# Two layers of long convolution and MLP: the first filter half loaded in quarters, the last MLP tile in two column pieces, and a new instruction order

## The chip, the cores and the metric

One core of one Trainium2 chip runs the whole program. The metric is device time in microseconds (us), lower is better. Engines: PE (TensorE), DVE (VectorE), ACT (ScalarE), POOL (GpSimd) and SP (SyncE, which here only issues DMAs).

## The reference, cut to what matters

```python
def _A_ref(q, k, v, shift_k, ssm_k, ssm_D):          # S = 2048 tokens, D = 512 channels
    for t in range(4):                                # a causal 4-tap filter along the tokens
        k_shift = k_shift + k_pad[:, t:t + S, :] * shift_k[:, 3 - t]
    kv = k_shift * v
    y = irfft(rfft(kv padded to 2S) * rfft(ssm_k padded to 2S))[:S]   # a long causal convolution per channel
    return q * (y + kv * ssm_D)

def _B_ref(x, w1, b1, w2, b2):                        # F = 1376
    return gelu(layernorm(x) @ w1 + b1) @ w2 + b2

x = A_q
x = x + _A_ref(layernorm(x), ...);  x = x + _B_ref(layernorm(x), ...)
x = x + _A_ref(layernorm(x), ...);  x = x + _B_ref(layernorm(x), ...)    # same weights
```

The convolution y does not depend on x, so it is computed once and used by both layers.

## The kernel before

The convolution is done as Fourier products by tables (Ft, Wt, Mt and Gt) on PE. Filter and input are cut into two halves of 1024 tokens, h = 0 and 1. A piece of work has a name, and the table ORDER lists all pieces, each with its engine (P for PE, A, D, G for POOL, S for SP) and its buffer (a PSUM slot 0 to 3 for a P piece). A piece is written out where the table puts it; each engine then runs its own pieces strictly in that order and waits by semaphores. A name that ends in e is the eviction from PSUM of the P piece before it, and the table says whether ACT or DVE does it. The pieces, with the half h as their first digit:

- lK: loads of the filter ssm_k (L391); KT: its transposes (L423); dt: adds ssm_D to one row. K0cSq: first stage of the filter's first half, 4 channel groups c by two parts q (L354); K0T: transposes of it (L368). The second half goes another way: K1S (L443), then K1w writes it to a buffer in DRAM and K1r reads it back regrouped (names zd; L382 and L388).
- lF, lW, lM, lG: loads of the tables Ft, Wt, Mt, Gt. lk: DMA transposes of the input k (L394). lv, lx, w1 to w4: loads of v, q and the weights.
- dg: diagonals for the 4-tap filter; kv: the filter as matmuls (L473); kvm: times v (DVE, L479).
- KW: second stage of the filter (L488); wa: a swap of its partitions by DMAs (L498). U0cSq, U0T and U1S, U1w, U1r: first stage of the input's two halves, made like the filter's. X: its second stage (L488). T, Ta, Tb: products with the filter on DVE (L547; they need X evicted, KW and wa). V: back transform (L558 for the first half, L572 for the second). The first half's V is transposed by TP (L589), the second's goes through DRAM (vw, vr). Y: the last stage (L603).
- For each of 8 token blocks i (two layers by four blocks of 512 tokens): sa and sb (statistics of the layernorm, DVE), pa, pb (its scale, POOL), aa, ab (applied, ACT or DVE), ga (gate by Y and sum, DVE), LT or dw and dr (transpose of the normed block on PE, or through DRAM by a DMA transpose, L674 and L677), m1 (first matmul of the MLP, L689), ge (gelu, ACT, L696), m2 (second matmul, four tiles of 128 tokens, 11 matmuls each, L706), re (sum with x, DVE, L710) and st (store, L719).

All DMAs named above go through SP's queue, one after the other; only of the last block's stores one half goes through ACT's queue.

At the start 38 matmuls on a zero tile (L322) keep PE busy while the first loads run.

Of the kernel before, what the change touches and what calls it, by code (L numbers as in the profile page):

```python
# [16 lines left out]
lK01.S lK00.S lF.S lG.S lK11.S lK10.S lk00.S KT01.P0 KT01e.D KT00.P1 dt1.D col.P0 KT00e.A K02S0.P2 cole.D K03S0.P3  # L17
K02S0e.D0 dg2.G KT11.P0 K03S0e.A1 K02S1.P1 KT11e.D lk01.S K03S1.P2 K02S1e.A KT10.P3 dt0.D dg1.G K03S1e.A K01S1.P1
KT10e.D K01S0.P0 K0T3.P2 K01S0e.A2 lv0.S K01S1e.D lW.S K00S0.P3 ones0.G K00S1.P0 lM.S dg0.G K00S0e.A1 K0T1.P1 lk10.S
K00S1e.D K0T3e.A K0T2.P3 K0T1e.D K0T0.P0 dg3.G K0T2e.D kv00.P2 K0T0e.A kv02.P1 kvm00.D kS.G KW03.P0 KW02.P3 kvm02.D  # L20
kv01.P2 KW02e.A lk11.S KW03e.A KW00.P1 kvm01.D U00S0.P3 KW00e.A KW01.P0 U00S0e.D1 kv03.P2 KW01e.A KW05.P1 kvm03.D
U02S0.P3 KW05e.A wa00.S U00S1.P0 U02S0e.A0 U03S0.P2 U00S1e.D U03S1.P1 U03S0e.A2 U01S0.P3 U03S1e.D U02S1.P0 U01S0e.A3
U01S1.P2 U02S1e.D KW06.P1 U01S1e.A KW07.P3 KW06e.D KW04.P0 U0T0.P2 KW04e.A U0T2.P1 KW07e.A U0T0e.D4 U0T1.P0 wa01.S
U0T2e.D5 X00.P2 X01.P3 U0T1e.D6 X00e.A U0T3.P1 X01e.A T00.D0 X02.P0 lx0.S K1S2.P2 X02e.A U0T3e.D0 X04.P3 w2.S K1S2e.A1
V00.P0 T01.D1 X06.P1 V00e.A X03.P2 X06e.D X03e.A X07.P0 X07e.A T02.D0 V01.P2 K1S6.P1 X04e.A T03.D1 V02.P0 V01e.A
K1S7.P3 T04.D0 K1S6e.A0 V03.P2 T06.D2 V02e.A X05.P1 X05e.A T07.D1 V04.P0 K1S7e.A V06.P1 T05.D0 V03e.A V07.P3 sa02.D
V06e.A V05.P2 lv1.S V07e.A K1S4.P1 sa10.D pa02.G K1w3.S V04e.A kv13.P3 sa00.D pa10.G V05e.A K1S5.P0 K1S4e.A5 TP01.P2
na02.D sa12.D pa00.G K1S5e.A TP00.P1 TP01e.A6 kvm13.D K1w2.S pa12.G TP02.P0 w1.S w3.S TP00e.D2 kv11.P3 TP02e.A0 aa00.D
Y01.P2 kv10.P1 kvm11.D aa02.A kv12.P0 kvm10.D Y01e.A Y00.P3 kvm12.D K1S0.P1 Y00e.A K1S3.P2 ga02.D K1S0e.A2 K1S1.P3
K1S3e.A ga00.D U1S0.P1 K1S1e.A TP03.P0 K1w1.S sb02.D U1S0e.A5 Y02.P3 K1w0.S w4.S U1S7.P2 Y02e.A sb00.D U1S6.P1 pb02.G  # L30
U1S6e.A0 U1S2.P3 TP03e.D6 pb00.G U1S7e.A U1S4.P1 ab02.D U1S2e.A1 U1S1.P0 U1w3.S K1r3.S ab00.D LT02.P2 U1S1e.A K1r1.S
na10.D LT02e.D LT00.P3 K1r0.S Y03.P0 na12.D aa10.A LT00e.D U1w0.S U1S3.P2 U1S4e.D6 m100.P3 U1S3e.A Y03e.D U1w1.S
U1S5.P2 ge00.A ga10.D m101.P1 aa12.A sb10.D m103.P3 ge01.A U1S5e.D pb10.G m102.P0 ge03.A ga12.D U1w2.S K1r2.S m104.P3
sb12.D ge02.A pb12.G KW16.P0 ge04.A m105.P2 KW16e.D U1r3.S6 KW10.P1 ge05.A KW11.P3 ab10.D KW13.P0 KW11e.A m201.P2
ab12.D dw10.S KW13e.A dw12.S U1r0.S1 KW10e.A KW15.P0 re01.D KW17.P3 KW15e.A KW14.P1 m200.P2 KW14e.D dr1.S KW17e.A
wa11.S X10.P3 re00.D KW12.P1 X16.P0 m203.P2 X16e.A0 sa20.D KW12e.A Tb16.D0 pa20.G X10e.A1 wa10.S m202.P1 Tb10.D1
re03.D m110.P3 aa20.D re02.D ga20.D m112.P1 ge10.A sa22.D U1r1.S5 m113.P3 ge12.A U1r2.S0 Ta16.D2 pa22.G lx1.S X11.P1
sb20.D V16.P2 X11e.A1 m114.P0 V16e.A1 Tb11.D0 pb20.G ge13.A aa22.D m111.P2 Ta10.D2 ge14.A nb20.D ga22.D V10.P3 ge11.A
X17.P0 Ta11.D1 m115.P1 V10e.A6 X12.P2 X17e.A1 Ta17.D2 V11.P3 X12e.A0 X14.P0 Tb17.D0 ge15.A X15.P2 Ta14.D1 X14e.A2
V17.P1 m210.P0 Tb14.D0 V17e.A X15e.A1 sb22.D vw13.S ab20.A V14.P2 Tb15.D2 pb22.G V11e.A m211.P1 Ta15.D0 V14e.A0 vw10.S  # L40
# [713 lines left out]
```

## Time and profile before

| | |
|---|---|
| time, three runs | 247.8, 247.82 and 248.97 us, median 247.82 |
| the profiled execution | 249.34 us, its span 247.6 us |
| busy in the span | PE 233.4, DVE 169.7, ACT 153.5, POOL 46.1 us |
| mean granted clock of PE | 0.989 |

The span runs from the first to the last instruction on the core; the time has some 1.7 us more around it. Matmuls overlap, so a PE that is shown busy need not be at its peak rate. Idle time of an engine is put down to whoever ended it. Of the lines numbered above, L266 is the eviction on ACT and L268 that on DVE.

### The profile page before, as it was taken

To read this page: it belongs to the slowest core of one execution; us is meant where nothing else is said; L and a number is where in the kernel's file an instruction comes from. 1 tells how busy PE (TensorE), PEld (TensorE's weight loads), DVE (VectorE), ACT (ScalarE), POOL (GpSimd) and SP (SyncE) were. 2 spreads that over 40 slices of the span, in tenths; PEclk is the share of its full clock that TensorE was granted. 3 is DMA by queue.
4 is the path that set the end of the run, shared out by engine and by line. 5 is a ranking of instruction groups with operands and counts; after the bars stand their busy time and mean duration, and the time that the engine had idled before them with its cause. 6 is when DMAs were issued, how large, how long until landed. Compare 5 with 4: busy or idle time off the path is not lost.

```text
span 247.6 us, 4645 instructions
## 1 busy us (share of the span) xinstructions
PE 233.4 (94%) x1852; PEld 122.7 (50%) x1852; DVE 169.7 (69%) x308; ACT 153.5 (62%) x197; POOL 46.1 (19%) x91
## 2 busy tenths in 40 slices
PE   8999997799899999988899999999999999999993
PEld 8997664585444344433343344444444444444441
DVE  0798899989998489999986996064886863001312
ACT  2678979989988745999329806794029521955000
POOL 1590000230202023304212550011132111000000
PEclk9999999999999999999799999999999999999998
DMA  6999979946599899936966152302401263300045
GB/s 211 263 265 243 206 160 220 376 160 230 217 274 360 255 232 207 290 67 184 230 196 211 45 127 96 75 3 85 86 0 45 77 134 88 82 3 0 0 115 139
DMA packets 41447, 38.72 MB, mean 156 GB/s; under 512 B 24556, under 2 KB 36306, under 8 KB 40402
## 3 DMA queue, kind: packets, MB, share of 16 engines
q1 hardware_dynamic: 41074, 38.17, 56.9%
q10 hardware_dynamic: 352, 0.27, 0.4%
q8 instruction: 14, 0.23, 0.4%
q14 instruction: 7, 0.06, 0.1%
HBM read 16.41 MB, written 12.06 MB: 115 GB/s over the span
## 4 chain that ended last, share of the span: by engine, by line
PE 78%; ACT 11%; DVE 5%; DMA 2%; issue 2%; POOL 1%; SPq 0%; DVEq 0%; ACTq 0%
PE p L689 31%; PE p L706 27%; ACT arena L266 10%; PE p L473 3%; PE p L368 3%; PE p L443 2%; PE p L572 2%; DMA arena<-zd 2%; DVE arena L268 2%; PE p L488 2%; PE p L322 2%; PE p L354 1%; PE p L423 1%; DVE arena L547 1%; PE p L589 1%
## 5 line engine op out<-in xcount | busy, mean ns | idle before, releaser
L266 ACT ACTIVATE arena<-p 128x1024 bf16<-128x1024 f32 (+1 forms) x79 | 79.8, 1103 | 15.5 <-PE p L488 6.1
L696 ACT ACTIVATE arena<-p,B 128x512 bf16<-128x512 f32 (+1 forms) x88 | 54.0, 686 | 43.6 <-PE p L689 43.5
L706 PE MATMUL p<-arena 128*128 128x512 bf16 (+1 forms) x352 | 78.9, 383 | 0.4 <-ACT arena L696 0.4
L689 PE MATMUL p<-arena 128*128 128x512 bf16 (+1 forms) x352 | 78.1, 379 | 0.0
L706 PEld LDWEIGHTS <-arena 128*128 128x128 bf16 (+1 forms) x352 | 34.2, 98 | 44.4 <-issue 4.7
L689 PEld LDWEIGHTS <-arena 128*128 128x128 bf16 (+1 forms) x352 | 34.7, 100 | 41.7 <-issue 1.9
L710 DVE TENSOR_TENSOR arena<-p,arena 128x512 bf16<-128x512 f32 x32 | 21.6, 685 | 43.6 <-PE p L706 24.1
L286 DVE BATCH_NORM_STATS2 lst<-arena 128x6 f32<-128x512 bf16 x64 | 40.8, 680 | 0.4
L293 POOL TENSOR_SCALAR lrs<-lmv 128x2 f32<-128x2 f32 x32 | 8.8, 276 | 148.6 <-DVE lmv L288 146.5
L547 DVE TENSOR_TENSOR arena<-arena 128x2048 bf16<-128x2048 bf16 x24 | 28.4, 1218 | 1.0 <-ACT arena L266 0.8
L304 ACT ACTIVATE arena<-arena,lnm,lrs 128x512 bf16<-128x512 bf16 x28 | 21.2, 809 | 11.9 <-DVE lnm L298 11.9
L295 POOL TENSOR_TENSOR lrs<-lrs,mhalf 128x2 f32<-128x2 f32 x32 | 25.9, 810 | 2.7
L655 DVE TENSOR_TENSOR arena<-arena 128x1024 bf16<-128x1024 bf16 x16 | 10.9, 681 | 13.8 <-ACT arena L304 11.8
L268 DVE COPY arena<-p 128x2048 bf16<-128x2048 bf16 (+1 forms) x13 | 14.5, 1136 | 8.2 <-PE p L423 6.6
L268 DVE CAST arena<-p 128x1024 bf16<-128x1024 f32 x14 | 16.7, 1217 | 1.8 <-PE p L488 0.9
L306 DVE TENSOR_SCALAR arena<-arena,lmv,lrs 128x512 bf16<-128x512 bf16 x36 | 13.1, 413 | 0.3 <-POOL lrs L295 0.2
L443 PE MATMUL p<-arena,Ft 128*128 128x512 bf16 x48 | 12.4, 380 | 1.0 <-ACT arena L266 0.7
L488 PE MATMUL p<-arena,Wt 64*64 64x512 bf16 x128 | 11.4, 391 | 1.9 <-ACT arena L266 1.0
L656 DVE TENSOR_TENSOR arena<-arena 128x1024 bf16<-128x1024 bf16 x16 | 11.1, 692 | 0.6
L572 PE MATMUL p<-arena 64*64 64x512 bf16 x128 | 9.0, 399 | 2.3 <-ACT arena L266 2.2
L456 POOL TENSOR_SCALAR arena<-IDt,sF 128x128 bf16<-128x128 bf16 x16 | 9.4, 604 | 7.6 <-DVE B L268 7.5
L479 DVE TENSOR_TENSOR arena<-p,arena 128x1024 bf16<-128x1024 f32 x8 | 9.6, 1222 | 1.6 <-PE p L473 1.4
(46 smaller groups left out, 123.1 us busy)
## 6 DMA issues: line engine op xcount, KB each, us to landing
arena<-arena SPq DMA_DIRECT2D x16, 256.0 KB, 4.1
zd<-arena SPq DMA_DIRECT2D x8, 512.0 KB, 5.2
arena<-zd SPq DMA_DIRECT2D x8, 512.0 KB, 5.9
lnd<-arena SPq DMA_DIRECT2D x14, 256.0 KB, 2.2
arena<-in_A_ssm_k_dram SPq DMA_DIRECT2D x4, 512.0 KB, 4.9
arena<-in_A_v_dram SPq DMA_DIRECT2D x2, 1024.0 KB
arena<-in_A_q_dram SPq DMA_DIRECT2D x4, 512.0 KB, 7.9
vd<-arena SPq DMA_DIRECT2D x8, 256.0 KB, 3.3
```

The costliest lines, as they stand in the source:

```text
L266: nc.scalar.activation(dst, src, AF.Copy)
L268: nc.vector.tensor_copy(dst, src)
L286: nc.vector.bn_stats(lst[:, i, :], xg[:, i, :])
L295: nc.gpsimd.tensor_tensor(self.rs[:, a:b], self.rs[:, a:b], mhalf[:, a:b], ALU.pow)
L304: nc.scalar.activation(dst[:, i, :], xg[:, i, :], AF.Identity, bias=self.nm[:, i:i + 1], scale=rs)
L443: nc.tensor.matmul(o[:, gh, :], Ft[:, t + gh, :], src[:, n, :], start=x == 0, stop=x == len(parts) - 1)
L488: nc.tensor.matmul(o[cols, par, :], Wt[rows, 2 * j + kk, :], z[rows, kk, :], start=True, stop=True)
L547: nc.vector.tensor_tensor(Tb[it["slot"]["T"]].rearrange("p s a d -> p s (a d)"), x2, kk, ALU.mult)
L689: nc.tensor.matmul(o[0:m, x, :], W1t[:, ct, ft * P:ft * P + m], lt[:, ct, :], start=ct == 0, stop=ct == CT - 1)
L696: nc.scalar.activation(ht[0:m, ft, :], o[0:m, x, :], AF.Gelu_apprx_tanh, bias=B1[0:m, ft:ft + 1])
L706: nc.tensor.matmul(o, ht[0:m, ft, t * P:t * P + P], W2t[0:m, ft, :], start=ft == 0, stop=ft == FT - 1)
L710: nc.vector.tensor_tensor(xg[:, t, :], view(pf[pe["slot"]["ps"]], [D]), xg[:, t, :], ALU.add)
```

## The change

1. The filter's first half comes in four loads of 128 channels (256 KB, before two of 512 KB), each with its own 8 transposes, its own eviction of 128x1024 and its own sum with ssm_D, so that a channel group of the first stage needs its own quarter alone.
2. The last block's tile t = 1 is made in two pieces of 256 columns, named x = 1 and x = 4, each with 11 matmuls, a sum and a store of its own. The piece of the first columns stands four tiles from the end, the other is the last of all.
3. 30 warm-up matmuls instead of 38.
4. A new table ORDER: other places for pieces on all engines, other engines for some evictions, and other PSUM slots.

```diff
-        for i in range(38):
+        for i in range(30):
             nc.tensor.matmul(pf[NPS - 1][:, 0:P], idle[:], idle[:], start=True, stop=True)
...
+        CW = [1, 2]
+        lK = [[load(f"lK{h}{x}", Kraw[h][:, x * CW[h]:(x + 1) * CW[h], :], ..., CW[h] << 18)
+               for x in range(CT // CW[h])] for h in range(2)]
...
+            w = CW[h]
+            for x in range(CT // w):
...
+                    for j in range(w):
                         for n in range(NT):
+                            nc.tensor.transpose(o[:, j, n, :], Kraw[h][:, w * x + j, n::NT], IDt[:])
...
-            zs = [first_stage("K0", Ktok[0], c, [KTe[0][c // 2]]) for c in range(CT)]
+            zs = [first_stage("K0", Ktok[0], c, [KTe[0][c]]) for c in range(CT)]
...
+            last = i == len(seq) - 1
+            for t, x, d0, d1 in [(0, 0, 0, D), (1, 1, 0, D // 2 if last else D), (2, 2, 0, D), (3, 3, 0, D)] + [(1, 4, D // 2, D)] * last:
+                def mms(it, t=t, ht=ht, d0=d0, d1=d1):
+                    o = view(pf[it["slot"]["ps"]], [d1 - d0])
...
+                        nc.tensor.matmul(o, ht[0:m, ft, t * P:t * P + P], W2t[0:m, ft, d0:d1], start=ft == 0, stop=ft == FT - 1)
...
+                def resid(it, pe=pe, xg=xg, t=t, d0=d0, d1=d1):
+                    nc.vector.tensor_tensor(xg[:, t, d0:d1], view(pf[pe["slot"]["ps"]], [d1 - d0]), xg[:, t, d0:d1], ALU.add)
...
+                            if d1 - d0 < D:
+                                o = apf(out, o.offset + d0, [list(o.ap[0]), list(o.ap[1]), [1, d1 - d0]])
+                                queue("A" if gh else "S").dma_start(o, xh[h][rows, n, d0:d1])
```

Of the table, one stretch on PE: the end of the second half's V pieces and the MLP tiles among them.

```diff
-V17.P1 m210.P0 Tb14.D0 ... V14.P2 ... m211.P1 ... V15.P2 X13.P3 ... V12.P2 ... V13.P2 m212.P3
+V17.P3 ... m211.P0 ... V14.P1 ... X13.P3 ... V15.P2 ab22.A m210.P1 ... V12.P2 re10.D ... V13.P2 m212.P1
```

First place, SP's queue from its first DMA to the swap of the first half. The names are those of the tensors: in_A_ssm_k is the filter, Ft, Gt, Wt and tabM the tables, in_A_k the input k, in_A_v the input v, and L498 the swap (wa). Before:

```order
L325 DMA arena<-in_A_ssm_k_dram 128x2x1024 x2
L325 DMA Ft<-tabF 128x768
L325 DMA Gt<-tabG 128x64
L325 DMA arena<-in_A_ssm_k_dram 128x2x1024 x2
L394 DMA_TRANSPOSE arena<-in_A_k_dram 128x4x512 x2
L325 DMA arena<-in_A_v_dram 128x4096
L325 DMA Wt<-tabW 128x1024
L325 DMA arena<-tabM 128x2048
L394 DMA_TRANSPOSE arena<-in_A_k_dram 128x4x512 x2
L498 DMA arena<-arena 32x4096 x8
```

The same stretch of SP's queue now, where the lines have moved by a few (L398 is the DMA transpose, L503 the swap):

```order
L326 DMA arena<-in_A_ssm_k_dram 128x1024 x4
L326 DMA Ft<-tabF 128x768
L326 DMA arena<-in_A_ssm_k_dram 128x2x1024 x2
L398 DMA_TRANSPOSE arena<-in_A_k_dram 128x4x512 x2
L326 DMA arena<-in_A_v_dram 128x4096
L326 DMA Wt<-tabW 128x1024
L398 DMA_TRANSPOSE arena<-in_A_k_dram 128x4x512
L326 DMA Gt<-tabG 128x64
L398 DMA_TRANSPOSE arena<-in_A_k_dram 128x4x512
L326 DMA arena<-in_B_b_dram 1x512
L326 DMA arena<-tabM 128x2048
L503 DMA arena<-arena 32x4096 x8
```

The filter's first half is four DMAs, Ft stands behind all four of them, and the table Mt (tabM) is moved from ahead of the second pair of transposes to the place right ahead of the swap.

Second place, DVE around the start of the MLP, from the eviction of the first block's second transpose (COPY 128x4x256, piece LT00e). CAST 128x1024 is an eviction, p0 to p3 the PSUM slots, L655 and L656 the gate, L286 and L288 statistics. Before:

```order
L268 COPY arena_63<-p3_156 128x4x256
L268 CAST arena_63<-p1_154 128x1024
L268 CAST arena_63<-p0_153 128x1024
L655 TENSOR_TENSOR arena_63<-arena_63 128x1024
L656 TENSOR_TENSOR arena_63<-arena_63 128x1024
L286 BN_STATS lst_87<-arena_63 128x6 x2
L288 BN_AGGR lmv3_97<-lst_87 128x2 x2
L268 CAST arena_63<-p2_155 128x1024
L655 TENSOR_TENSOR arena_63<-arena_63 128x1024
L656 TENSOR_TENSOR arena_63<-arena_63 128x1024
```

The same place now (L269 the eviction, L660 and L661 the gate):

```order
L269 COPY arena_63<-p0_153 128x4x256
L299 SCALAR_TENSOR_TENSOR lnm2_96<-lmv2_94,lrs2_95 128x2
L269 CAST arena_63<-p1_154 128x1024
L660 TENSOR_TENSOR arena_63<-arena_63 128x1024
L661 TENSOR_TENSOR arena_63<-arena_63 128x1024
L287 BN_STATS lst_87<-arena_63 128x6 x2
L289 BN_AGGR lmv3_97<-lst_87 128x2 x2
L660 TENSOR_TENSOR arena_63<-arena_63 128x1024
L661 TENSOR_TENSOR arena_63<-arena_63 128x1024
```

Three evictions (U1S4e, Y03e, U1S5e) have left this place for ACT, and one (Y02e) has come.

Third place, DVE's last five rows, the sums of the last tiles. Before:

```order
L710 TENSOR_TENSOR arena_63<-p2_155,arena_63 128x512 x2
L710 TENSOR_TENSOR arena_63<-p3_156,arena_63 128x512
L710 TENSOR_TENSOR arena_63<-p0_153,arena_63 128x512 x2
L710 TENSOR_TENSOR arena_63<-p3_156,arena_63 128x512
L710 TENSOR_TENSOR arena_63<-p2_155,arena_63 128x512
```

And now:

```order
L717 TENSOR_TENSOR arena_63<-p3_156,arena_63 128x512 x2
L717 TENSOR_TENSOR arena_63<-p2_155,arena_63 128x512
L717 TENSOR_TENSOR arena_63<-p0_153,arena_63 128x256
L717 TENSOR_TENSOR arena_63<-p3_156,arena_63 128x512
L717 TENSOR_TENSOR arena_63<-p0_153,arena_63 128x256
```

The last sum is of 256 columns, and the other piece of that tile stands one row ahead of the last whole one.

125 lines of the change are left out of this document (59 added, 66 removed).

## The prediction

> **What bounds the kernel now.** I read the page first (shares and clock), then the busy time by stage, then the chain of work that ended last, and then the timeline at the places where the chain leaves PE.
>
> ```profile
> span 247.6 us, 4645 instructions
> PE 233.4 (94%) x1852; PEld 122.7 (50%) x1852; DVE 169.7 (69%) x308; ACT 153.5 (62%) x197; POOL 46.1 (19%) x91
> ```
>
> The 94% of PE is a mean over stages. The next view cuts the span where the chain changes; each row gives a stretch, its length, and busy us (and instructions) of PE, weight loads, DVE, ACT and POOL, then the granted clock, the DMA share and GB/s.
>
> ```profile
> 20.87:49.89 29.02, 25.06 (x477) 16.96 (x476) 27.91 (x32) 27.00 (x30) 1.79 (x4) 1.00 0.96 234
> 49.89:69.42 19.53, 18.61 (x206) 12.13 (x205) 17.82 (x36) 18.50 (x20) 3.52 (x8) 1.00 0.58 203
> 69.42:80.75 11.33, 11.33 (x63) 5.00 (x62) 10.25 (x18) 9.61 (x16) 1.76 (x4) 1.00 0.92 315
> 80.75:118.85 38.10, 34.79 (x273) 14.71 (x271) 33.23 (x51) 29.25 (x36) 8.11 (x8) 1.00 0.83 206
> 118.85:138.67 19.82, 19.39 (x99) 7.84 (x98) 16.80 (x42) 11.06 (x18) 6.07 (x12) 0.91 0.66 190
> 138.67:243.41 104.74, 104.73 (x484) 47.59 (x483) 51.07 (x118) 46.15 (x73) 14.02 (x29) 1.00 0.26 66
> 243.41:247.60 4.19, 0.00 (x0) 0.00 (x0) 0.69 (x1) 0.00 (x0) 0.00 (x0) 0.76 0.43 127
> ```
>
> From 138.67 on PE runs 484 MLP matmuls without a gap, 104.74 us, 0.216 each. No order makes that shorter. What can move is the time at which PE reaches that stretch, and the 4.19 us behind it. Ahead of it DVE and ACT are the full engines: from 20.87 to 49.89 they are busy 27.91 and 27.00 of 29.02, and from 20.87 to 118.85 DVE works 27.91 + 17.82 + 10.25 + 33.23 = 89.2 of 98.0 us. DVE's last product of the convolution (piece Tb13) ends at 118.85, and the last V piece starts on PE 0.06 later, as the chain (start, length, what) shows:
>
> ```profile
> 1.05 4.24 PE p L322 x38
> 5.28 1.62 PE p L423 x16
> ...
> 8.54 1.04 PE p L354 x8
> 9.57 0.99 PE p L423 x16
> ...
> 116.73 1.08 PE p L572 x16
> ...
> 118.91 1.59 PE p L572 x16
> 120.51 5.96 PE p L706 x22
> ...
> 138.67 9.67 PE p L706 x44
> ```
>
> So I read the change by one question: when does DVE finish Tb13, and does PE then run through.
>
> **Term 1, the head (filter loads and first stage).** Rows of the timeline (SP's issues, the first 4-tap products on DVE, the first second-stage matmuls on PE) and of the DMA issues (size, us from issue to landing):
>
> ```profile
> 1.81 0.47 SPq L325 DMA_DIRECT2D Ft<-tabF  x1
> 14.08 0.42 SPq L325 DMA_DIRECT2D Wt<-tabW  x1
> 19.35 2.36 DVE L479 TENSOR_TENSOR arena<-p,arena 128x1024 bf16<-128x1024 f32 x2 [0.60 <-PE p L473]
> 20.14 0.63 PE L488 MATMUL p<-arena,Wt 64*64 64x512 bf16 x8
> ...
> Wt<-tabW SPq DMA_DIRECT2D x1, 256.0 KB, 5.6
> Ft<-tabF SPq DMA_DIRECT2D x1, 192.0 KB, 4.9
> ```
>
> Now the first stage starts at 8.54, after 16 transposes (1.62), their eviction and the corner sum. With quarters, 30 warm-ups of 4.24 / 38 = 0.11 end at 4.4 and 8 transposes at 0.1 end at 5.2; but the first stage also needs Ft. Ft lands at 1.81 + 4.9 = 6.7, behind 1 MB of filter in both orders. Four quarters of transposes and their first evictions fill PE until about 7.3, so the first stage starts some 1.2 earlier. Two more evictions and corner sums on DVE cost 0.2 of it, which leaves 1.0 for the 4-tap products on DVE (19.35). The second stage gets less: Wt lands at 14.08 + 5.6 = 19.7, the same bytes ahead of it, and PE starts it at 20.14 now, so its lead cannot pass 0.45. I take -0.6; bounds 0 and -1.0. The 8 warm-ups taken out (0.9 us of PE) are inside this: the landing of the loads covers them.
>
> A page's rule on these warm-ups: the Trainium skill, "TensorE: Matmul & The Clock Gate", section "Part 1: The HAM clock gate (the "warmup" mystery)", says PE starts at half rate and is released after a free-running window of about 3.4 us of sustained work. The rows agree so far: the first 16 transposes take 1.62, a later 16 take 0.99. By that rule 30 warm-ups alone would be too short to fill a window, and the sum would be -3.4 instead of -4.0 if the loads leave a hole; in the sum itself nothing of this is used.
>
> **Term 2, work taken off DVE.** By the order, between the first 4-tap product and Tb13 DVE loses three evictions net: one in the input's first stage (five became four) and two at the start of the MLP (of five, three left and one came, and one of KW's moved between engines both ways). The sum of one MLP tile (piece re10) is moved ahead of Tb13. Prices:
>
> ```profile
> 26.95 3.47 DVE L268 CAST arena<-p 128x1024 bf16<-128x1024 f32 x3
> ...
> L710 DVE TENSOR_TENSOR arena<-p,arena 128x512 bf16<-128x512 f32 x32 | 21.6, 685 | 43.6 <-PE p L706 24.1 <-ACT arena L696 19.5
> L479 DVE TENSOR_TENSOR arena<-p,arena 128x1024 bf16<-128x1024 f32 x8 | 9.6, 1222 | 1.6 <-PE p L473 1.4
> L268 DVE COPY arena<-p 128x1024 bf16<-128x1024 bf16 x2 | 1.4, 688 | 0.0
> ```
>
> Three evictions in a row take 3.47; one sum 0.69: -3.47 + 0.69 = -2.8. DVE was idle 98.0 - 89.2 = 8.8 in this stretch, and I leave that as it is; if it grows by as much as was taken off, the term is 0, and if the better fit also takes a third of the idle time away, it is -5.7. I take -2.8, because the row that it rests on is the full engine's own. What hides the three evictions on ACT is ACT's idle time: 98.0 - (27.00 + 18.50 + 9.61 + 29.25 = 84.4) = 13.6.
>
> The next one late could be a DMA. The second half's X pieces wait at 87.15 for the input read back from DRAM:
>
> ```profile
> 82.08 0.59 SPq L388 DMA_DIRECT2D arena<-zd  x1
> 87.15 0.84 PE L488 MATMUL p<-arena,Wt 64*64 64x512 bf16 x12 [0.47 <-DMA arena<-zd]
> ...
> 74.09 1.20 DVE L268 CAST arena<-p 128x1024 bf16<-128x1024 f32 x1
> ```
>
> That read is issued at 82.08, after SP has stored the block's normed rows. The last eviction of the input's first stage (74.09 on DVE, U1S5e) is one of those that are moved ahead of the MLP, and the two gates behind it on DVE come sooner by the evictions taken out, so this DMA moves with DVE and does not keep the gain.
>
> **Term 3, behind Tb13.** Between 115 and 125 the clock falls:
>
> ```profile
> 115.00:120.00 5.00, 2.80 (x47) 1.28 (x36) 5.00 (x7) 3.62 (x5) 0.00 (x0) 0.93 0.70 208
> 120.00:125.00 5.00, 5.00 (x24) 1.84 (x17) 5.00 (x15) 1.02 (x1) 2.64 (x6) 0.73 0.99 240
> ```
>
> PE has 2.20 idle here, and then 16 V matmuls take 1.59 instead of 1.08 and 22 MLP matmuls 5.96 instead of 9.67 / 2 = 4.84: 1.6 lost to the clock. Now an MLP tile (piece m210, 11 matmuls, 9.67 / 4 = 2.4) stands between the V pieces there, ahead of the two that wait longest. If that keeps the clock up, up to 1.6 is won. But something else is late next. The following block's normed rows come by a DMA transpose:
>
> ```profile
> 143.76 1.87 SPq L677 DMA_TRANSPOSE arena<-lnd  x1
> arena<-lnd SPq DMA_TRANSPOSE x7, 4.3
> ```
>
> It lands at 143.76 + 4.3 = 148.1, and PE begins that block at 138.67 + 9.67 = 148.3. There is no slack, so PE can gain behind Tb13 only what that chain gains, and DVE, which carries it, is busy 16.80 of 19.82. I take -0.7, near the middle of 0 and -1.6. The same page and section say that the rate falls back after a whole idle window; here PE was busy 2.80 of the 5.00 us and the clock fell all the same (0.93, then 0.73), so the row decides; by the page there would be no dip to remove, and the sum would be -3.3.
>
> **Term 4, the end.** The last sum is on 256 columns. The rows for 512 and 1024 columns (685 and 1222 ns) give 537 ns per 512, so 256 cost 685 - 268 = 417: -0.27. The split adds 11 matmuls but no columns (8 of 256 columns take 1.04 with their tail, 0.11 each, half of 0.216). The store is half as large; it lands 2.5 after its issue now, and for its size I count nothing.
>
> ```profile
> out_dram<-arena ACTq DMA_DIRECT2D x4, 64.0 KB, 2.5
> ```
>
> I take -0.3; bounds -0.2 and -0.4.
>
> **Term 5, a wait added.** The table Mt now stands ahead of the swap in SP's queue.
>
> ```profile
> 24.66 3.14 SPq L498 DMA_DIRECT2D arena<-arena  x4
> 34.41 1.22 DVE L547 TENSOR_TENSOR arena<-arena 128x2048 bf16<-128x2048 bf16 x1
> ...
> arena<-arena SPq DMA_DIRECT2D x16, 256.0 KB, 4.1
> ```
>
> The swap lands at 24.66 + 3.14 + 4.1 = 31.9, and the first product on DVE needs it at 34.41, which terms 1 and 2 (one eviction of the three) move to about 32.7. Mt's 512 KB at 234 GB/s (stage row) are 2.2 us. If all of that comes ahead of the swap, it lands at 34.1 and DVE waits 1.4; but the transposes of k no longer queue behind Mt and all of the bytes are the same, so most is given back. I take +0.4; bounds 0 and +1.4. The q load behind the swap is in this too.
>
> **Sum:** -0.6 - 2.8 - 0.7 - 0.3 + 0.4 = -4.0. The profiled execution took 249.34 with its span of 247.6, so it would become 245.3; it lies 1.5 above the median of the runs, 247.82, which would become 243.8.
>
> **The rivals.**
> - *The added wait and the DMA chain take most of it.* Term 5 in full (+1.0 more) and term 3 at 0 (+0.7): -2.3, 245.5. For it speaks the DMA share of 0.96 in the stage, against it that the bytes do not change. A late clock release at the head (0.6 lost, 244.4) lies on the way to it.
> - *The new order does not do what it says:* DVE's idle time grows by what was taken off, and Wt stops the head. Then the end and a part of the head stay: 247.82 - 0.3 - 0.4 = 247.1. The 8.8 idle us are made of many short waits, which another order can as well make longer.
> - *Slower: ACT becomes the engine that sets the first MLP.* The evictions taken off DVE, and the second normed pair of the next block, now stand on ACT ahead of the first gelu:
>
> ```profile
> 71.35 1.27 ACT L696 ACTIVATE arena<-p,B 128x512 bf16<-128x512 f32 x2 [0.66 <-PE p L689]
> 72.50 1.51 ACT L304 ACTIVATE arena<-arena,lnm,lrs 128x512 bf16<-128x512 bf16 x2
> ```
>
>   ACT is busy 18.50 of 19.53 from its last V eviction (49.89) to the first MLP matmul. The three evictions, priced as on DVE, and the pair are 3.47 + 1.51 = 5.0 more ahead of the gelu. Free are 1.03 there and the 0.66 that the first gelu waits. The pair is no longer between the gelus, 1.5 back. If ACT gets to its last V eviction at the old time, PE reaches the second matmul 5.0 - 1.7 - 1.5 = 1.8 later, and the end is at 247.82 + 1.8 - 0.3 = 249.3. It decides when ACT's lead at that eviction is under 1.5. Against it: ACT was idle 2.0 from 20.87 to 49.89 (29.02 - 27.00), and the head's lead arrives there.
>
> **How the numbers follow.** A difference under 0.5% (1.24 us) cannot be told from no change. Forecast, 241.9 to 244.9, chance 0.56. The wait and the chain, 244.9 to 246.6, 0.20. Only a rest stays, 246.6 to 249.0, 0.15. ACT bound, above 249.0, 0.09. Faster than 246.6: 0.56 + 0.20 = 0.76; within, 0.15; slower, 0.09. The low end is term 2 at -3.8 and term 3 at -1.6 with the others as taken, -5.9: 241.9. The high end, 247.1, is where the third case is half held; above it lie about 0.16, below the low end about 0.04.
>
> **What would show it.** DVE's last product (the last L547 row, now L552) ends near 115.4 instead of 118.85; no row of clock under 0.9 between 110 and 125; the stretch of MLP matmuls without a gap begins near 135 and is as long as before; the last sum takes 0.42; the first stage begins near 7.3. Wrong would be: a first product on DVE waiting for the swap by over 1 us, ACT without a gap up to a first gelu later than 71, or PE idle for a DMA transpose behind 138.

## The result, and the profile after

The changed kernel takes 246.48 us (median of 5, 246.03 to 246.93), the kernel before 248.47 on the same chip (median of 5): a ratio of 0.9899, 95% interval 0.9863 to 0.9935. Medians are of all executions; ratios, here and below, leave out those more than 1.5% above the fastest of their kernel. The profiled execution of after took 246.79.

The head of its page, and its time by stage (start:end, length, busy us and instructions of PE, weight loads, DVE, ACT and POOL, granted clock, DMA share, GB/s), cut at the same events as before:

```profile
span 245.1 us, 4654 instructions
...
PE 230.9 (94%) x1855; PEld 122.6 (50%) x1855; DVE 165.1 (67%) x308; ACT 156.8 (64%) x202; POOL 46.9 (19%) x91
```

```profile
22.22:50.25 28.03, 25.33 (x476) 16.84 (x472) 25.68 (x27) 27.13 (x30) 0.68 (x2) 1.00 0.92 237
50.25:70.28 20.03, 18.33 (x214) 12.75 (x213) 19.20 (x41) 19.45 (x21) 4.64 (x11) 1.00 0.71 249
70.28:81.18 10.90, 10.90 (x62) 4.79 (x60) 9.08 (x19) 10.65 (x18) 3.19 (x5) 1.00 0.87 301
81.18:118.53 37.35, 35.05 (x273) 14.77 (x271) 32.63 (x50) 29.17 (x36) 8.05 (x8) 1.00 0.86 215
118.53:136.72 18.19, 17.75 (x98) 7.49 (x98) 17.01 (x45) 11.05 (x18) 6.02 (x12) 1.00 0.67 187
136.72:241.49 104.77, 104.76 (x495) 48.73 (x494) 50.47 (x114) 46.57 (x73) 13.99 (x29) 1.00 0.30 69
241.49:245.10 3.61, 0.00 (x0) 0.00 (x0) 0.43 (x1) 0.00 (x0) 0.00 (x0) 0.91 0.23 55
```

DVE is busy 4.6 less than before and ACT 3.3 more: the evictions that changed engine (of those of 128x1024 f32, DVE does 10 instead of 14 and ACT 78 instead of 74). The gapless MLP stretch starts at 136.72 instead of 138.67 and is as long as before (104.77 and 104.74). The first row starts 1.35 later than before, at 22.22. The fifth row is 1.63 shorter and has a clock of 1.00 where it had 0.91. The last is 0.58 shorter.

The timeline of after, at the head and at the end (start, length, engine, line, what, and in brackets how long the engine sat idle and for what):

```profile
0.80 1.86 SPq L326 DMA_DIRECT2D arena<-in_A_ssm_k_dram  x4
...
4.50 10.56 SPq L398 DMA_TRANSPOSE arena<-in_A_k_dram  x2
...
7.08 0.60 PE L355 MATMUL p<-Ft,arena 128*128 128x256 bf16 x4
...
15.11 0.58 SPq L326 DMA_DIRECT2D arena<-in_A_v_dram  x1
...
21.11 3.73 DVE L484 TENSOR_TENSOR arena<-p,arena 128x1024 bf16<-128x1024 f32 x3 [1.60 <-DMA arena<-in_A_v_dram]
...
241.52 0.43 DVE L717 TENSOR_TENSOR arena<-p,arena 128x256 bf16<-128x256 f32 x1 [0.51 <-PE p L713]
241.97 0.53 SPq L728 DMA_DIRECT2D out_dram<-arena  x1
```

The first stage starts on PE at 7.08, before at 8.54. But the first 4-tap product on DVE starts at 21.11, before at 19.35, and DVE has waited 1.60 for v. SP issued v at 15.11, before at 13.44, since the two DMA transposes of k ahead of it took 10.56 of the queue; before they took 8.07. The same two rows before:

```profile
5.33 8.07 SPq L394 DMA_TRANSPOSE arena<-in_A_k_dram  x2
...
13.44 0.58 SPq L325 DMA_DIRECT2D arena<-in_A_v_dram  x1
```

From that product to the gapless stretch after needs 136.72 - 21.11 = 115.61, before 138.67 - 19.35 = 119.32. So the profiles differ by +1.76 at the head, -3.71 in the middle and -0.58 at the end.

### The profile page after: what moved, and what is told of

Read it like the earlier page. It is cut to its first block, busy times and chain, and to the rows that moved or that the text cites. A ratio compares the mean times of both kernels' runs of the same rounds, so it can differ in the third digit from the quotient of the medians.

```text
span 245.1 us, 4654 instructions
## 1 busy us (share of the span) xinstructions
PE 230.9 (94%) x1855; PEld 122.6 (50%) x1855; DVE 165.1 (67%) x308; ACT 156.8 (64%) x202; POOL 46.9 (19%) x91
## 4 chain that ended last, share of the span: by engine, by line
PE 77%; DVE 6%; DMA 5%; SPq 5%; ACT 4%; issue 2%; DVEq 0%; ACTq 0%
PE p L713 31%; PE p L694 31%; SPq L398 4%; DVE arena L552 4%; PE p L478 3%; ACT arena L267 3%; PE p L448 2%; DMA arena<-in_A_v_dram 2%; PE p L577 2%; PE p L493 2%; DMA zd<-arena 2%; PE p L369 1%; PE p L594 1%; PE p L355 1%; DMA arena<-in_A_ssm_k_dram 1%
## 5 line engine op out<-in xcount | busy, mean ns | idle before, releaser
L267 ACT ACTIVATE arena<-p 128x1024 bf16<-128x1024 f32 (+2 forms) x84 | 83.3, 1098 | 13.2 <-PE p L493 5.7
L713 PE MATMUL p<-arena 128*128 128x512 bf16 (+3 forms) x363 | 77.8, 373 | 0.5 <-ACT arena L701 0.4
L694 PE MATMUL p<-arena 128*128 128x512 bf16 (+1 forms) x352 | 77.9, 380 | 0.0
L713 PEld LDWEIGHTS <-arena 128*128 128x128 bf16 (+1 forms) x363 | 35.1, 97 | 42.3 <-issue 2.6
L694 PEld LDWEIGHTS <-arena 128*128 128x128 bf16 (+1 forms) x352 | 34.8, 100 | 41.6 <-issue 2.0
L717 DVE TENSOR_TENSOR arena<-p,arena 128x512 bf16<-128x512 f32 (+1 forms) x33 | 21.5, 667 | 49.9 <-PE p L713 39.0
L294 POOL TENSOR_SCALAR lrs<-lmv 128x2 f32<-128x2 f32 x32 | 10.0, 314 | 145.8 <-DVE lmv L289 141.9
L269 DVE COPY arena<-p 128x2048 bf16<-128x2048 bf16 (+1 forms) x14 | 14.9, 1070 | 10.5 <-PE p L428 7.2
L660 DVE TENSOR_TENSOR arena<-arena 128x1024 bf16<-128x1024 bf16 x16 | 10.9, 683 | 4.4 <-ACT arena L305 2.5
L269 DVE CAST arena<-p 128x1024 bf16<-128x1024 f32 x10 | 12.0, 1217 | 2.0 <-ACT arena L701 1.6
L661 DVE TENSOR_TENSOR arena<-arena 128x1024 bf16<-128x1024 bf16 x16 | 11.1, 692 | 0.6
```

The lines of the kernel that those rows point to most:

```text
L267: nc.scalar.activation(dst, src, AF.Copy)
L269: nc.vector.tensor_copy(dst, src)
L694: nc.tensor.matmul(o[0:m, x, :], W1t[:, ct, ft * P:ft * P + m], lt[:, ct, :], start=ct == 0, stop=ct == CT - 1)
L713: nc.tensor.matmul(o, ht[0:m, ft, t * P:t * P + P], W2t[0:m, ft, d0:d1], start=ft == 0, stop=ft == FT - 1)
L717: nc.vector.tensor_tensor(xg[:, t, d0:d1], view(pf[pe["slot"]["ps"]], [d1 - d0]), xg[:, t, d0:d1], ALU.add)
```

## The experiments

Every profile below is read by the same two marks: the start of the first 4-tap product (the head) and the distance from it to the gapless stretch (the middle). "Ratio" is to the kernel before on the same chip.

**The three evictions back on DVE.**

```diff
-U1S4e.A1 ... U1S5e.A ... Y03e.A
+U1S4e.D1 ... U1S5e.D ... Y03e.D
```

> The changed kernel with the three evictions U1S4e, U1S5e and Y03e done by DVE again instead of ACT. Theory 1 (term 2: DVE is the full engine, each eviction of 1.16 on it is on the path): DVE's last product of the convolution ends 1.5 to 3.5 later than 118.53, the gapless MLP stretch starts 1.5 to 3.5 later than 136.72, and the time is 248.0 to 250.0. Theory 2 (ACT is as full, so that what DVE loses ACT had gained): the last product ends within 0.7 of 118.53, and the time stays at 246.0 to 247.2.

Measured: 249.47, ratio 1.0044 (1.0022 to 1.0067), 3.0 more than after. Its timeline and its chain of work:

```profile
20.45 2.36 DVE L484 TENSOR_TENSOR arena<-p,arena 128x1024 bf16<-128x1024 f32 x2 [1.13 <-DMA arena<-in_A_v_dram]
...
119.80 1.21 DVE L552 TENSOR_TENSOR arena<-arena 128x2048 bf16<-128x2048 bf16 x1
```

```profile
137.88 1.27 ACT arena L701 x2
139.15 0.04 issue
139.20 0.81 PE p L713 x3
```

The last product starts 2.48 later than in after (117.32), with a head 0.66 sooner. The middle is 139.20 - 20.45 = 118.75, 3.14 longer than in after, for three evictions priced at 3.47. Theory 1 holds: they stood on the path, and ACT had room for them. The clock is not the cause: seven of the twelve executions have a mean clock of 0.992 or less, but the other five, at 0.998 or more, have a median of 249.28.

**The MLP tile as a filler, alone in the kernel before.**

```diff
-V14.P2 Tb15.D2 pb22.G V11e.A m211.P1 Ta15.D0 ... vw12.S V12.P2
+V14.P2 Tb15.D2 pb22.G V11e.A Ta15.D0 ... vw12.S m211.P1 V12.P2
```

> The kernel before with one MLP tile (piece m211, 11 matmuls, 2.4 us on PE) moved from ahead of the V piece V14e's neighbour to right ahead of V12, so that PE has work while DVE makes the last products. Theory 1 (term 3: the clock drop behind Tb13 comes from PE's idle time of 2.2 us ahead of it): the clock rows of 115 to 125 rise from 0.93 and 0.73 to 0.98 or more, and the gapless stretch starts 1.0 to 1.6 sooner than 138.67, at 137.1 to 137.7; the time falls by as much from 248.5. Theory 2 (the drop has another cause, or the DMA transpose of the next block sets the end of this stretch anyway): the stretch starts within 0.5 of 138.67 and the time stays within 0.5 of the kernel before, whether or not the clock rises.

Measured: 248.82 against 248.68, ratio 1.0005 (0.9977 to 1.0033). In its profile the clock does rise, by the time in 5-us windows:

```profile
115.00:120.00 5.00, 3.82 (x38) 1.77 (x41) 4.45 (x6) 3.41 (x4) 0.00 (x0) 1.00 0.73 213
120.00:125.00 5.00, 4.95 (x33) 2.12 (x23) 5.00 (x14) 1.03 (x1) 2.62 (x6) 1.00 1.02 219
```

Its gapless stretch starts at 137.53, 1.14 sooner than in the profile of before. The times do not follow, as theory 2 has it for the time, while the stretch starts where theory 1 has it. The next experiment shows why.

**The four loads alone, in the kernel before.** The first half comes in four loads with four transposes and sums; nothing else moves.

```diff
-lK01.S lK00.S lF.S lG.S lK11.S lK10.S lk00.S
+lK02.S lK03.S lK00.S lK01.S lF.S lG.S lK11.S lK10.S lk00.S
```

> The kernel before with the filter's first half in four loads, its transposes in four pieces, and nothing else changed (the order of the rest, the 38 warm-up matmuls' successor count and the tail as before). Theory 1 (the four loads slow what stands behind them): the second filter half lands at 11.8 or later instead of 10.6, the first 4-tap product starts 1.0 or more later than 19.1 to 19.4, the time grows by 0.5 to 1.5 from 248.5. Theory 2 (quarters alone cost nothing behind them): it starts within 0.4 of 19.2, and the time stays within 0.6 of the kernel before.

Measured: 248.91 against 248.08, ratio 1.0033 (1.0002 to 1.0064). Timeline at the head, then the same 5-us windows:

```profile
5.63 7.75 SPq L396 DMA_TRANSPOSE arena<-in_A_k_dram  x2
...
19.11 2.35 DVE L482 TENSOR_TENSOR arena<-p,arena 128x1024 bf16<-128x1024 f32 x2 [0.61 <-PE p L476]
```

```profile
115.00:120.00 5.00, 2.79 (x52) 1.32 (x44) 5.00 (x6) 3.91 (x5) 0.00 (x0) 1.00 0.72 211
120.00:125.00 5.00, 5.00 (x31) 2.20 (x24) 5.00 (x14) 1.02 (x1) 2.65 (x6) 1.00 1.05 225
```

The head is at 19.11: four loads in the old order delay nothing at the head, as theory 2 has it. The time is 0.83 longer, which is theory 1's range; this profile has no place for that loss, and it stays unexplained. And PE is busy 2.79 of 5.00, as in the profile of before, with no filler, yet the clock stays at 1.00. The middle is 137.67 - 19.11 = 118.56. Its chain shows what comes next when the clock does not fall: PE gets through to 126.65 and then waits for the second half's V, read back from DRAM.

```profile
126.65 3.89 DMA arena<-vd
```

**The split last tile alone, in the kernel before,** its two pieces as the last two.

```diff
-m270.P0 st23.S st73.S m271.P2 re70.D st51.S re72.D st70.S st72.S re71.D st71.S
+m270.P0 st23.S st73.S m271.P2 re70.D st51.S re72.D st70.S st72.S m274.P3 re71.D st71.S re74.D st74.S
```

> The kernel before with its last MLP tile alone in two pieces of 256 columns, the second of them the last of all, and nothing else changed. Theory 1 (term 4 as predicted: only the shorter last sum counts): the stretch behind the last matmul is 3.9 instead of 4.19, and the time falls by 0.3. Theory 2 (the smaller store lands sooner too, as the changed kernel's profile shows): it is 3.5 to 3.7 and the time falls by 0.5 to 0.7. Theory 3 (the split costs PE as much, 11 more matmuls of half the columns with a gap): the gapless stretch is 0.3 or more longer and the time does not change.

Measured: 248.92 against 248.08, ratio 1.0025 (1.0000 to 1.0051). By windows, and by the timeline of the end:

```profile
115.00:120.00 5.00, 2.79 (x40) 1.39 (x36) 5.00 (x7) 3.58 (x5) 0.00 (x0) 0.90 0.72 211
120.00:125.00 5.00, 5.00 (x25) 1.81 (x18) 5.00 (x15) 1.02 (x1) 2.65 (x6) 0.76 0.98 234
...
243.72:247.70 3.98, 0.00 (x1) 0.00 (x0) 0.42 (x1) 0.00 (x0) 0.00 (x0) 1.00 0.37 105
```

```profile
242.36 1.36 PE L707 MATMUL p<-arena 128*128 128x256 bf16 x11 [0.17 <-DVE arena L711]
...
243.76 0.42 DVE L711 TENSOR_TENSOR arena<-p,arena 128x256 bf16<-128x256 f32 x1 [1.11 <-PE p L707]
244.25 1.18 SPq L722 DMA_DIRECT2D out_dram<-arena  x2
```

Behind the last matmul 3.98 are left, not 3.61. The two stores of 32 KB stand one after the other on SP (1.18), so the second waits for the first, and PE waits 0.17 for a buffer. The stretch behind the last matmul is near theory 1's 3.9, but the gapless stretch is 0.35 longer (138.63 to 243.72), and the time does not fall: theory 3. The changed kernel has the first piece four tiles from the end; that place alone, in the old order, was not run.

**Mt back behind Wt.**

```diff
-lW.S dg0.G ... KW00e.A lM.S U02S0.P1
+lW.S lM.S dg0.G ... KW00e.A U02S0.P1
```

> The changed kernel with the load of Mt moved back to its old place, right behind Wt and ahead of the last two DMA transposes of k. Theory 1 (term 5 of the prediction: Mt ahead of the swap delays it): the swap lands up to 0.4 sooner, the first product of the convolution starts by 36.0 instead of 36.33, and the time falls by 0.4 or less. Theory 2 (the swap is held by the evictions of the filter's second stage, not by Mt): the swap is issued at 27.0 as now and the time stays within 0.3 of 246.5. Theory 3 (the DMA queues are full from 20 to 27): the last transposes of k, now behind Mt, come later, and the time grows by up to 1.0.

Measured: 246.26, ratio 0.9914 (0.9883 to 0.9945). The first issues of the swap (timeline), first in this version:

```profile
27.09 3.14 SPq L503 DMA_DIRECT2D arena<-arena  x4
```

And in after:

```profile
27.01 3.28 SPq L503 DMA_DIRECT2D arena<-arena  x4
```

Mt ahead of the swap costs nothing: in after Mt is issued by 25.57, and the swap comes 1.44 later, when an eviction on ACT is done. Here the queue is not free before 26.97, since the transposes of k come later. The first product is 0.45 sooner (35.88), which theory 1 has too, but only because the head is (20.65): from the head to it are 15.23, in after 15.22. So it is theory 2, with the queue in the place of the evictions in this one version.

**Plain loads ahead of the DMA transposes of k.**

```diff
-lK11.S lk00.S ... lk01.S ... lv0.S ... lW.S
+lK11.S lv0.S lW.S lk00.S lk01.S
```

> The changed kernel with two lines of SP's queue moved: the plain loads of v and Wt stand ahead of the two DMA transposes of k, which stood ahead of them. Theory 1 (the head is late because the DMA transposes start while plain loads still wait, and the mixture is slow): v lands before 17 instead of 20.99, Wt before 19 instead of 21.66, the first 4-tap product starts by 19.5 instead of 21.11, the first product of the convolution by 34.8 instead of 36.33, and the time falls by 1.0 to 2.0, to 244.5 to 245.5. Theory 2 (the queue carries the same bytes in any order, the quarters or Ft behind them are what costs): the wait only changes from v to k, the first 4-tap product stays at 21 or later, and the time stays within 0.5 of 246.5.

Measured: 247.07, ratio 0.9953 (0.9924 to 0.9982). Timeline:

```profile
20.43 2.90 PE L478 MATMUL p<-arena 64*128 64x256 bf16 x32 [2.44 <-DMA arena<-in_A_k_dram]
...
22.36 1.22 DVE L484 TENSOR_TENSOR arena<-p,arena 128x1024 bf16<-128x1024 f32 x1 [3.11 <-PE p L478]
```

PE now waits 2.44 for k where DVE waited for v, and the head is 1.25 later. A part of that is the clock: this profiled execution (249.35) is one of three in twelve with a mean clock of 0.993 or less, and by windows of 1 us its clock is 0.50 from 21 to 24, so that 44 matmuls of the filter take 3.54 instead of 2.15. Theory 1 falls; it is theory 2's exchange of one wait for another, and a little worse than that in time.

**Gt back in its old place, alone and with Mt.**

```diff
-lF.S lK10.S lK11.S lk00.S
+lF.S lG.S lK10.S lK11.S lk00.S
```

> The changed kernel with one small load (the table Gt, 16 KB) moved back to its old place on SP's queue, between Ft and the filter's second half. Theory 1 (with Gt there the queue issues the last filter load at 5.2 and the first DMA transpose at 5.6 instead of 4.0 and 4.5, as in the kernel before with quarters, so that transposes do not mix with plain loads): the second filter half lands at 10.4 to 10.7 instead of 12.1, v at 18.9 to 19.3 instead of 20.3 to 21.0, the first 4-tap product starts at 19.1 to 19.5, and the time falls by 1.0 to 2.0 to 244.5 to 245.5. Theory 2 (Gt's place does not matter, the landing differs for another reason): the second half lands at 11.8 or later, the first 4-tap product starts at 20.4 or later, and the time is within 0.5 of 246.5.

> Both moves on SP's queue together in the changed kernel: Gt back between Ft and the filter's second half, and Mt back right behind Wt. Theory 1 (the head's lateness is all that the new queue order costs): time 244.3 to 245.3, the first 4-tap product at 19.1 to 19.5 and the first product of the convolution by 34.8. Theory 2 (the swap, which waits for the evictions of the filter's second stage, sets the first product whatever the head does): the first 4-tap product comes at 19.1 to 19.5, the first product of the convolution at 35.5 or later, and the time is 245.8 to 246.5.

Measured: 246.27, ratio 0.9918 (0.9889 to 0.9947), and 246.08, ratio 0.9920 (0.9891 to 0.9948). Timeline of the version with Gt alone:

```profile
4.98 9.72 SPq L398 DMA_TRANSPOSE arena<-in_A_k_dram  x2
...
20.42 2.36 DVE L484 TENSOR_TENSOR arena<-p,arena 128x1024 bf16<-128x1024 f32 x2 [1.22 <-DMA arena<-in_A_v_dram]
```

The head comes 0.69 sooner than in after, and DVE still waits 1.22 for v: by the numbers this is theory 2. That the 0.69 is Gt's is not shown, since versions with Gt late have their head at 20.65 (Mt early) and 20.45 (evictions back). With Mt as well the head is at 20.15, later than either theory had it, the first product at 35.39, between the two, the middle 115.70, and the time in theory 2's band.

**Two loads instead of four in the changed kernel, alone and with Mt behind Wt.**

```diff
-lK00.S lK02.S lK01.S lK03.S lF.S lK10.S lK11.S lk00.S
+lK00.S lK01.S lF.S lK10.S lK11.S lk00.S
```

> The changed kernel with the filter's first half in two loads of 512 KB again (two evictions less at the head, the rest of the new order kept). Theory 1 (the four loads make the second filter half land late: 12.0 to 12.2 in four profiles with quarters, 10.6 in two profiles without): the second filter half lands by 11.0, the first 4-tap product starts by 19.9 instead of 20.5 to 21.1, and the time falls by 0.5 to 1.5 against the changed kernel's 246.5. Theory 2 (it is the order on SP's queue, where the DMA transposes of k are issued at 4.5 instead of 5.3, that costs): the second half still lands at 11.8 or later, the first 4-tap product stays at 20.4 or later, and the time is 246.2 to 247.2.

> The changed kernel with the filter's first half in two loads again, and Mt right behind Wt. With two loads the profile of the changed order should show what the quarters do. Theory 1 (quarters let the queue run ahead, so that DMA transposes mix with plain loads; two loads hold it back): the second filter half lands by 11.0, the first 4-tap product starts by 19.9, the time is 245.0 to 246.0. Theory 2 (the head is as late, and the gain of the version with two loads comes from the two evictions and sums less on ACT and DVE): the first 4-tap product starts at 20.4 or later, and the time is 245.0 to 246.0 all the same.

Measured: 245.79, ratio 0.9905 (0.9878 to 0.9932), whose profiled execution stalled (1313 us) and is read only for the pair of transposes; and 245.82, ratio 0.9919 (0.9892 to 0.9947). Timeline of the second:

```profile
5.09 7.05 SPq L397 DMA_TRANSPOSE arena<-in_A_k_dram  x2
...
20.05 2.36 DVE L483 TENSOR_TENSOR arena<-p,arena 128x1024 bf16<-128x1024 f32 x2
```

The transposes take 7.05 of the queue instead of 10.56 (7.10 in the first version, ahead of its stall), and v is there in time (no bracket: DVE came straight from its other work). The head is at 20.05, which fits a first stage that begins at 7.96 instead of 7.08. By the head it is near theory 1 of the second expectation (20.05 against 19.9), and the second filter half lands at 10.2 as that has it.

**The second filter half loaded behind Wt and Mt,** with its two transposes and evictions moved back as well.

```diff
-lF.S lK10.S lK11.S lk00.S ... KT10.P0 ... KT10e.D ... KT11.P1 ... KT11e.A
+lF.S lk00.S ... lW.S lM.S lK10.S lK11.S ... U01S1.P2 KT10.P0 U03S1e.D KT10e.D ... KW04.P0 KT11.P3 kS.G ... KW04e.A KT11e.A
```

> The changed kernel with the loads of the filter's second half (1 MB, first used at 39.7) moved from ahead of the DMA transposes of k to behind Wt and Mt, with their transposes and evictions moved behind the first half's input stage, and the second half's DMA transposes of k behind the last swap. Theory 1 (the head waits for the bytes ahead of v and Wt, whatever their order): v and Wt land 3 to 4.5 sooner than 20.5 to 21.7, the first 4-tap product starts at 16 to 18, the first product of the convolution at 33 or sooner instead of 36.3, and the time falls by 1.5 to 4, to 242.5 to 245. Theory 2 (the moved transposes and evictions land in the stretch where DVE and ACT are full, and give back what the head gains): the first 4-tap product comes as early, but the first product stays at 35.5 or later, and the time is 246 to 248.

Measured: 251.02, ratio 1.0110 (1.0065 to 1.0155). Timeline of DVE, and the stretch from the first 4-tap product's place to the first product of the convolution:

```profile
17.60 1.22 DVE L484 TENSOR_TENSOR arena<-p,arena 128x1024 bf16<-128x1024 f32 x1
...
35.26 1.22 DVE L269 COPY arena<-p 128x2048 bf16<-128x2048 bf16 x1 [2.86 <-PE p L369]
...
38.20 1.22 DVE L552 TENSOR_TENSOR arena<-arena 128x2048 bf16<-128x2048 bf16 x1
```

```profile
17.00:38.20 21.20, 18.55 (x248) 14.83 (x245) 14.83 (x13) 14.97 (x16) 0.81 (x3) 0.92 0.50 126
```

The head is 3.5 sooner, and the first product 1.9 later (36.33 in after). Two transposes that filled idle PE time at the head now stand where PE is busy 18.55 of 21.20, and DVE waits 2.86 for PE. A part of this wait is the clock, 0.92 in the stretch and 0.50 from 32 to 34 by windows of 1 us; but the one execution with a mean clock of 1.00 took 251.02 too. Worse than theory 2 thought: what waits at the head also uses its waiting time.

**Three loads: two quarters and a half.**

```diff
-lK00.S lK02.S lK01.S lK03.S lF.S lK10.S lK11.S lk00.S KT00.P0 KT00e.D KT02.P1 KT02e.A dt0.D KT01.P0 KT03.P2 KT01e.A
+lK00.S lK01.S lK02.S lF.S lK10.S lK11.S lk00.S KT00.P0 KT00e.D KT01.P1 KT01e.A dt0.D KT02.P2
```

> The changed kernel with the filter's first half in three loads: two quarters and then one half (channel groups 2 and 3 together), their transposes and first stages in the order 0, 1, 2, 3, and Mt right behind Wt. It is to join the early first stage of the quarters (7.1) to the early landing of the second filter half that the version with two loads shows (10.2 instead of 11.6 to 12.2). Theory 1 (fewer DMAs ahead of the DMA transposes land sooner): the second filter half lands by 11.0, the first 4-tap product starts at 19.0 to 19.6 instead of 20.1 to 21.1, the gapless MLP stretch starts 115.7 after it, and the time is 244.5 to 245.4. Theory 2 (the number of loads does not set the landing): the second half lands at 11.5 or later, the first 4-tap product starts at 20.0 or later, and the time is 245.6 to 246.5.

Measured: 247.10, ratio 0.9919 (0.9878 to 0.9961). Its profiled execution took 245.26. Timeline and chain:

```profile
4.04 9.05 SPq L397 DMA_TRANSPOSE arena<-in_A_k_dram  x2
...
19.61 2.36 DVE L482 TENSOR_TENSOR arena<-p,arena 128x1024 bf16<-128x1024 f32 x2
```

```profile
133.91 1.27 ACT arena L699 x2
135.19 0.04 issue
135.23 0.81 PE p L711 x3
```

The profile has theory 1's head at the edge of its range, 19.61, and a middle of 135.23 - 19.61 = 115.62, but the median does not: 6 of its 12 executions have a mean clock of 0.984 to 0.993 and a median of 248.75, the others 245.72. No version here has a ratio below the interval of the changed kernel's own, so none is shown to beat it.

## Why the prediction was right, and where it was not

The forecast of 243.8 came 2.7 too low: 2.0 in the terms (-4.0 forecast, -2.0 measured) and 0.65 in the base, the median of the kernel before, 247.82 of three executions then and 248.47 of five now. 246.48 lies in the range, but in the band of the first rival. Of what that rival named, term 3 at 0 came; the wait that was added came too, but for v at the head and not for the swap. That the range holds the time is partly luck: it rests on term 2, while term 1 had the wrong sign and left its own bounds, and term 3 was counted twice. The terms, where "clean" is the old order with the clock at 1.00 (the filler and the four-loads versions, with a middle of 118.39 and 118.56):

| term | predicted | measured |
|---|---|---|
| 1, the head | -0.6 | +1.76 between the two profiles, +1.3 over three of each kind |
| 2, work off DVE (head to the end of Tb13) | -2.8 | -2.08 between the two profiles, -2.6 against clean; undoing the three evictions +3.14 |
| 3, behind Tb13 | -0.7 | -1.63 between the two profiles, -0.15 and -0.34 against clean |
| 4, the end | -0.3 | -0.58 |
| 5, Mt ahead of the swap | +0.4 | 0 |

**Term 1 failed, in sign.** The first stage did begin sooner, at 7.08, 0.2 better than worked out, and it was worth nothing; no cost of the 8 warm-ups left out shows there. The failed step is "the same bytes ahead of it": I let Wt and v land when they did and so bounded the head at 0 and -1.0. The bytes were the same (but for Gt's 16 KB), but the queue's time was not: the DMA transposes of k were issued from 4.50 and took 10.56. The issue of that pair, how long SP had waited ahead of it for a filter load to land, and the head:

| version | SP's wait | issue of the pair | ends | first 4-tap product |
|---|---|---|---|---|
| before | 1.4 | 8.07 | 13.40 | 19.35 |
| four loads, old order | 1.2 | 7.75 | 13.38 | 19.11 |
| after | 0.4 | 10.56 | 15.06 | 21.11 |
| after, Gt early | 0.6 | 9.72 | 14.70 | 20.42 |
| after, two loads, Mt early | 1.7 | 7.05 | 12.14 | 20.05 |
| after, three loads, Mt early | 0.4 | 9.05 | 13.09 | 19.61 |

Neither the four loads nor the new order alone delays v; together they do. The traces say more on why. In every profile with the same bytes ahead of the pair, where SP had waited 1.2 to 2.0 for a filter load (the old order, and the new one with two loads) the pair took 7.05 to 8.66, and where it had waited 0.4 to 0.7 (the new order with four or three) 9.05 to 10.56. That fits theory 1 of the second two-loads version: four loads in the new order let the queue run ahead. From 5.5 to 7.5 the DMA engines moved 189 GB/s in after, against 312 before and 336 with four loads in the old order. No run changed SP's wait alone, so that the wait is the cause is not shown; and the time of the issue doesn't decide by itself, since three loads began it at 4.04 and ended it sooner than after. How large the term is depends on the execution, too: the three profiles of the old order with two loads have heads of 19.14, 19.35 and 19.80, the three with after's loads 20.45, 20.65 and 21.11, +1.3 in the mean.

The head matters in full. In after and in the versions with Mt early, Gt early, Gt and Mt early, two loads, and three loads, the middle is 115.61, 115.74, 115.79, 115.70, 115.66 and 115.62: what the head loses or wins arrives unchanged at the gapless stretch. In the old order it is not so: heads from 19.11 to 19.80 gave an end of Tb13 between 118.82 and 119.19, not in the same order, and all four chains pass through the read of zd that PE waits for until about 87; the chain of after doesn't.

**Term 2 was right in mechanism, and a little large.** DVE is the full engine up to Tb13, and three evictions less are 3.14 by the experiment that undoes them, against 3.47 from the rows. ACT took them. From the head to the end of Tb13 after needs 97.42, before 99.50, the clean versions 100.03 and 100.05: -2.08 and -2.6, where -2.8 was forecast. DVE's last product ends at 118.53 and not near 115.4: 2.4 of that is the head (+1.76 instead of -0.6), 0.7 this term. The sign named for the rival in which ACT sets the first MLP did come: ACT has no gap from 59.24 on, and its first gelu starts at 74.19, 2.8 later than before. But nothing waited for it: PE runs the first matmuls of the MLP from 70.28 without a gap (10.90 of 10.90), 0.9 later than before with a head 1.8 later.

**Term 3 rested on an accident of the profiled execution.** The dip of the clock is real there: behind Tb13 before needs 19.82, the clean versions 18.34 and 18.53, so it costs 1.3 to 1.5 of the 1.63. But the profile of before was one of those executions that have it. Of 93 executions of the kernel before beside the experiments (one stalled one left out), 24 have a mean clock of 0.993 or less and a median of 249.35; the other 69 have 0.996 or more and a median of 248.02. Before's profile belongs to the first kind (0.989, 249.34). I carried the 1.5 between it and the median through the sum as a constant, while term 3 took 0.7 out of the same 1.5: counted twice. The median of all 93 is 248.33, so that the term could win 0.3 there at most; the filler alone won nothing (1.0005). Whether a filler makes the dip rarer is not shown: 1 of 12 executions with it has such a clock, against 24 of 93.

The page's rule that I weighed (the Trainium skill, "TensorE: Matmul & The Clock Gate", section "Part 1: The HAM clock gate (the "warmup" mystery)") has the rate fall after an idle window of about 3.4 us, in windows that run free of the kernel. The fall itself came at less idle time than that (2.21 us in the split-tile version, clock 0.90 and then 0.76; in before 2.20, in gaps of 1.12 at most), so on the length the measurement decides; that the same idle time gave 1.00 in the four-loads version agrees with windows whose phase differs from one execution to the next.

The clock records in the traces show the windows. In the four profiles with a dip the clock first rises at 6.66 (before), 6.39 (split tile), 6.98 (plain loads first) and 3.97 (second half late), and from there to the fall are 33, 33, 4 and 8 times 3.413 us; each dip lasts 3.413 us. Counted from the rise, the window ahead of before's fall (115.89 to 119.30) holds nearly all of PE's two gaps, 1.96 idle. In the four-loads version the clock rises at 5.32, a window ends at 117.96 between the same two gaps, and the windows hold 1.09 and 1.12. So whether the two gaps cost anything depended on where the windows lay in that execution.

**Term 4** was mis-sized by 0.3. The sum is 0.43, as worked out (0.42). What I had put at nothing is the store: from its issue to the end 245.10 - 241.97 = 3.13, before 3.46 (244.17 to 247.63) with twice the bytes. That the bytes make the difference is not shown: in the split-tile version the last stores are as small, and 3.98 are left.

**Term 5** was 0: with Mt ahead of it the swap waited for an eviction, and was issued 5.90 behind the head in after (27.01); without, 6.44 behind it in the version with Mt early (27.09).

Measured terms against the clean old order, whose heads are at 19.11 and 19.14: +2.0 - 2.6 - 0.25 - 0.58 = -1.4; with the mean of +1.3 for the head, -2.1. The medians say -2.0 against the executions of before on the same chip (248.47), and -1.5 against the 69 at full clock.

## What to carry to other kernels

Before a dip, a wait or a slow stretch of the profiled execution is booked as something to win, ask whether the median execution has it; the distance between the two is the first hint, and a term must not be taken out of a distance that is carried along. Work taken off the engine that is full in a stage is worth nearly its own duration (3.14 of 3.47 here). "The same bytes ahead" doesn't fix when a load lands: on a queue with DMA transposes, look at how long the queue's issue takes, and what the queue waited for ahead of it.

## What the runs showed of the hardware that I had not expected

- The issue of the same two DMA transposes held SP's queue for 4.9 us (3.49 to 8.43 with the second filter half moved behind them) to 12.1 (5.79 to 17.91 with v and Wt ahead of them). What differs between these two is the plain bytes ahead of them, 1.2 and 3.4 MB; but at the same 2.2 MB it was 7.05 to 10.56, so the bytes are not all of it.
- The same stretch with PE busy 2.79 or 2.80 of 5.00 us kept the clock at 1.00 in one profile and let it fall to 0.73 and 0.76 in the window behind it in two others.
- Counted in windows of 3.413 us from the first rise, the clock of all 13 whole profiles changed only at the end of a window. It fell to 0.50 behind windows in which PE was idle for 1.66, 1.96, 2.20 and 2.44 us, and at the end of the program; it never fell where PE was idle for 1.63 or less, and of the few windows with 1.77 to 1.89 none was followed by a fall. So about half of a window idle is enough, and where the limit lies exactly the runs do not show. A dip takes half of 3.413, 1.7 us of PE's work.
- Two of the four dips lie far ahead of Tb13: at 20.63 in the version with plain loads first, behind PE's wait of 2.44 for k, and at 31.27 in the version with the second filter half late.
- None of 48 executions of the changed kernel and its versions with Gt, Mt, both, or two loads has a mean clock below 0.997, against 24 of 93 before with 0.993 or less. But the version with the three evictions back on DVE has that in 7 of 12, the one with three loads in 6 of 12, the one with plain loads first in 3 of 12, and the one with the second filter half late in 4 of 5. Where the clock falls in the first two, no profile shows. The profile with the evictions back has a window with 1.63 idle (64.34 to 67.75), but no fall.
